# The first chunk's layer norm ahead of k's transposes, its token pairs inline, and its two turned tiles given to two engines

## The chip, the core and the metric

The kernel runs on one core of a Trainium2 chip. The metric is the time of one execution in microseconds (us). TensorE (PE in the profile) multiplies matrices and also transposes tiles by multiplying with an identity; its weight loads are listed apart as PEld. VectorE (DVE), ScalarE (ACT) and GpSimd (POOL) do the elementwise work, and SyncE (SP) and POOL issue the transfers (DMAs) that matter here. Each engine works through its own queue in order; engines wait for each other by semaphores.

## The reference

The program is a forward and a backward pass of a small network on x of 2048 tokens by 448 features, in bf16. Two layers, A and B, are each applied twice:

```
x = A_q
x = x + A(layernorm(x), A_k, A_v, A_shift_k, A_ssm_k, A_ssm_D)
x = x + B(layernorm(x), B_w1, B_w2)
x = x + A(layernorm(x), ...)          # the same weights again
x = x + B(layernorm(x), B_w1, B_w2)

A(q, k, v, ...):  k_shift = causal filter of k with 4 taps per feature
                  kv = k_shift * v
                  y  = long convolution of kv with ssm_k (2048 taps per feature, by FFT) + kv * ssm_D
                  return q * y
B(x, w1, w2):     silu(x @ w1) @ w2                       # 448 -> 1792 -> 448
```

The outputs are x and the gradients of A_q, A_k, A_v, A_shift_k, A_ssm_k, A_ssm_D, B_w1 and B_w2 for a given gradient of x. The convolution result Y does not depend on x, so it is computed once and used by both applications of A. The first application of A and the norm in front of B are, for every token, `na = layernorm(x)`, `X = x + na * Y`, `nb = layernorm(X)`.

## The kernel before

**Stages.** `_ssm_prefix` (L280) computes Y in about the first 105 us. After it, `Main.run` (L717) does the two layers forward and most of the backward pass, and `_ssm_suffix` the rest. The prefix is the part in which most of the change lies, and everything in `Main` needs its Y.

**The prefix, in order.** Tokens lie as 128 partitions by 16 (`J`), so that token 16p + j stands on partition p; a spectrum tile has 112 column groups of 128 (`SPEC`, 14336 columns), worked in 14 chunks of 1024 (`NCI`).

1. Loads: SP issues ssm_k in four pieces (`K_sb`), the FFT matrix `M1sb` and k (`kn`, which borrows the tile `Ysb`) in halves, v (`v_n`), and the inverse matrix `Minvsb`, 17.2 us from issue to landing for that last one. Then ssm_k is transposed (L334) and goes through stage one of the FFT (L211) into `A1K`.
2. k's transposes (L352 to L360): four groups of PSUM tiles `ps_kT`, each copied half by ACT and half by DVE into `kT`, which lies inside the tile `KB`.
3. The convolution loop (L404 to L415): eight rounds (two feature halves h, four token groups jq). In each, `conv` does the four-tap filter as 128-row matmuls with diagonal matrices (`ps_cv`, L371), ACT copies the result to `ks` (L373), POOL stores it to `KS_d`, and DVE multiplies with v to `kvt` (L377). `stage1_kv` (L381) takes the round before through stage one: two PSUM tiles, four copies into `A1kv`. In the first four rounds `turn` (L346) also transposes 16 tiles of `A1K` at a time and copies them to `Z` (two turns a round, 1.2 us on DVE or 1.9 on ACT each); in the last four `_fft_stage2` works on K's spectrum instead (two chunks of 1024 a round, copied to `Z` by `cons_ka`).
4. K's spectrum: POOL stores it to DRAM (`spec_K`), and `_swap_halves_dma` (L240) copies it, with its two halves of partitions exchanged, into `KB`: 14 transfers of 256 KB, written `KB<-Z` in the profile. They can start only when `kT`, which lies in `KB`, is no longer read. The last conv's reads and the last product with `v_n` are also what the loads of `w2sb` and, after `M1sb`, of `w1sb` wait for, since these reuse the buffers.
5. **The norm of the first chunk** (L421 to L424): POOL issues the load of the first four token columns of A_q (`x0c0`), and `_ln` normalises them into `na0`. `_ln` (L252) does, for four columns `tl`, a `bn_stats` (L259; with `pin` these are held in program order) and a `bn_aggr` on DVE, then adds epsilon (`ln_ve`, DVE), raises to the power -1/2 on POOL (`rstd`, L266), forms minus mean times rstd on DVE (`ln_nmr`, L268), and applies scale and bias per column (L273 on ACT, or a DVE instruction); last, POOL stores the result to `N_d`.
6. `A1kv` is turned into `Zkv` (which lies in `A1K`) in seven groups, and for each of 14 chunks `cons_prod` copies the spectrum of kv (ACT or DVE, in the profile `A1K` L111 or L113, from `ps_s`), multiplies it on DVE with K's spectrum (`pa`, L443) and with its swapped form (`pb`, L444), POOL stores every second chunk to `spec_KV`, and two chunks later PE takes the products through inverse stage two (`ps_v`, L231 and L232), whose result is copied to `A1kv`.
7. Inverse stage one (`ps_y`, L461): eight groups, copied to `Ysb` (the first by DVE, the rest by ACT).

**The first chunk in Main.** Under high priority, `a_fwd` makes `a_t1` = na0 * Y and X = x0c0 + a_t1 in two pairs of token columns, `b_pre` normalises X the same way (all on DVE) to `nb`, and `b_tr` turns it by 16 PE transposes in two tiles `ps_t`, each copied to a half of `nT`. Then `h` starts the MLP's first matmuls (`ps_h`, L519), which read `nT`.

**What sets the order.** The tile framework's scheduler orders the instructions into the queues by priority and modelled times; nothing is written out by hand here but the `pin` and the high priority. Which engine makes a copy is decided while the program is built: `bal.pick` (L93) adds an estimated cost to the less loaded of ACT and DVE, so moving or re-costing one item shifts later choices. Copies are recorded at L111 (ACT) and L113 (DVE) whoever calls for them. PSUM tiles of the prefix come from one ring of four (tag "A"); a PE group that takes the next buffer waits until the copy out of its former contents is done.

Of the kernel before, what the change touches and what calls it, by code (L numbers as in the profile page):

```python
# [11 lines left out]
BF16 = mybir.dt.bfloat16  # L12
ACT = mybir.ActivationFunctionType
ALU = mybir.AluOpType
# [3 lines left out]
P = 128  # L18
S = 2048
D = 448  # L20
# [88 lines left out]
def _copy(nc, eng, out, in_):  # L109
    if eng is nc.scalar:  # L110
        nc.scalar.copy(out, in_)  # L111
    else:
        eng.tensor_copy(out, in_)  # L113
# [101 lines left out]
def _fft_stage2(k, Zt, psum, consume, chunks=range(NCI)):  # L215
    nc = k.nc
    Zf = (Zt if isinstance(Zt, bass.AP) else Zt[:]).rearrange("q a b -> q (a b)")
    for ci in chunks:
        ps = psum.tile([P, 1024], FP32, name="ps_s2", **k.pt["s2"])
        for hh in range(2):  # L220
            c0 = ci * 1024 + hh * 512
            nc.tensor.matmul(ps[:, hh * 512:(hh + 1) * 512], lhsT=k.Gsb[:, G_FWD, :], rhs=Zf[:, c0:c0 + 512], start=True, stop=True)
        consume(ci, ps)
# [24 lines left out]
def _pm(ap2d):  # L248
    return ap2d.rearrange("(p j) d -> p j d", j=J)


def _ln(k, pool, c, src, si, n_g, groups=((0, 4),), pin=False, eng=None):  # L252
    nc = k.nc
    for lo, hi in groups:
        n = hi - lo
        st = pool.tile([P, 4, 6], FP32, name="ln_st", tag="ln_st", bufs=1)
        mv = pool.tile([P, 4, 2], FP32, name="ln_mv", tag="ln_mv", bufs=2)
        for tl in range(lo, hi):
            i = nc.vector.bn_stats(out=st[:, tl, :], in_=src(tl))  # L259
            if pin:  # L260
                k.tc.keep_in_program_order(i)
            nc.vector.bn_aggr(out=mv[:, tl, :], in_=st[:, tl, :])
        ve = pool.tile([P, 4], FP32, name="ln_ve", tag="ln_ve", bufs=2)
        nc.vector.tensor_scalar(out=ve[:, 0:n], in0=mv[:, lo:hi, 1], scalar1=EPS, scalar2=None, op0=ALU.add)
        r = k.rstd[si][:, 4 * c:4 * c + 4]
        nc.gpsimd.tensor_tensor(out=r[:, lo:hi], in0=ve[:, 0:n], in1=k.mhalf[:, 0:n], op=ALU.pow)  # L266
        nmr = pool.tile([P, 4], FP32, name="ln_nmr", tag="ln_nmr", bufs=2)
        nc.vector.scalar_tensor_tensor(out=nmr[:, lo:hi], in0=mv[:, lo:hi, 0], scalar=-1.0, in1=r[:, lo:hi], op0=ALU.mult, op1=ALU.mult)  # L268
        k.bal.add("dve", 0.8 * n + 0.2)
        for tl in range(lo, hi):  # L270
            e = eng or k.bal.pick(D, act_ns=1.04, dve_ns=0.55, act_fixed=0.28)
            if e is nc.scalar:
                nc.scalar.activation(n_g[:, tl, :], src(tl), ACT.Identity, bias=nmr[:, tl:tl + 1], scale=r[:, tl:tl + 1])  # L273
            else:
                nc.vector.tensor_scalar(out=n_g[:, tl, :], in0=src(tl), scalar1=r[:, tl:tl + 1], scalar2=nmr[:, tl:tl + 1], op0=ALU.mult, op1=ALU.add)
    if si != 2:
        nc.gpsimd.dma_start(out=_pm(k.N_d[si][:])[:, 4 * c:4 * c + 4, :], in_=n_g[:])


def _ssm_prefix(k):  # L280
    nc, tc = k.nc, k.tc
# [3 lines left out]
    with ExitStack() as es:  # L285
        spec = es.enter_context(tc.tile_pool(name="spec", bufs=1))
        work = es.enter_context(tc.tile_pool(name="pwork", bufs=2))
# [41 lines left out]
        for dc in range(ND):  # L329
            kview = ksb[dc].rearrange("p (n1 n2) -> p n2 n1", n2=16)  # L330
            pt = psum.tile([P, 2, 1024], BF16, name="ps_kt", **a_)
# [14 lines left out]
        def turn(src, dst, g):  # L346
# [2 lines left out]
                nc.tensor.transpose(pt[:, i, :], src[:, 16 * g + i, :], k.ident[:])  # L349
            _copy(nc, bal.pick(2048, dve_ns=0.53), dst[:, 16 * g:16 * g + 16, :], pt[:])  # L350

        for jq in range(4):  # L352
            pt = psum.tile([DC, ND, 4, P], BF16, name="ps_kT", **a_)
            for u in range(4):
                j = 4 * jq + u
                for dc in range(ND):
                    nc.tensor.transpose(pt[:, dc, u, :], kn[:, j, dc * DC:(dc + 1) * DC], k.ident[:])
            for e, lo, hi in ((nc.scalar, 0, 2), (nc.vector, 2, 4)):
                _copy(nc, e, kT[:, jq, lo:hi, :, 1:129], pt[:, lo:hi])
# [57 lines left out]
            _swap_halves_dma(k, KB, Ka, 2048 * i, 2048 * (i + 1), nc.gpsimd)  # L417
        stage1_kv(*prev)
        _fft_stage2(k, Z, psum, cons_ka, range(8, NCI))

        k.x0c0 = k.dp.tile([P, 4, D], BF16, name="x0c0", tag="dstat", bufs=3)  # L421
        nc.gpsimd.dma_start(out=k.x0c0[:], in_=_pm(k.A_q[0])[:, 0:4, :])
        k.na0 = k.dp.tile([P, 4, D], BF16, name="na0", tag="dstat", bufs=3)
        _ln(k, work, 0, lambda tl: k.x0c0[:, tl, :], 0, k.na0, pin=True)  # L424


        B1 = A1kv[:].rearrange("p a c n s -> p a (c n s)")
        Zf = A1K[:].rearrange("p a c n s -> p (a c n s)")
# [36 lines left out]
class Main:  # L465
# [52 lines left out]
            seen[u] = seen.get(u, 0) + 1  # L518
            self.nc.tensor.matmul(ps[:, u, :], lhsT=w[lo:hi, b, f:f + P], rhs=x[lo:hi, b, :], start=(seen[u] == 1), stop=(seen[u] == ND))  # L519

    def transp(self, src, dst):
        nc, k = self.nc, self.k
        blocks = [(0, 128), (128, 256), (256, 384), (320, 448)]
        rows = P
        for h in range(2):
            pt = k.psum.tile([P, 2, 512], BF16, name="ps_t", tag="tr", bufs=2)
            for u in range(2):
                lo, hi = blocks[2 * h + u]
                for tl in range(4):
                    nc.tensor.transpose(pt[:rows, u, tl * P:(tl + 1) * P], src[:, tl, lo:hi], k.ident[:])  # L530
            _copy(nc, k.bal.pick(1024, dve_ns=0.53), dst[:rows, 2 * h:2 * h + 2, :], pt[:rows])

    def a_fwd(self, c, si, xc, n_g=None, groups=((0, 4),)):
        nc, k, X = self.nc, self.k, self.X
        if n_g is None:
            n_g = self.ch.tile([P, 4, D], BF16, name="na", tag="na", bufs=2)
            src = (lambda tl: xc[:, tl, :]) if xc is not None else (lambda tl: X[:, 4 * c + tl, :])
            _ln(k, self.ch, c, src, si, n_g)
        t1 = self.ch.tile([P, 4, D], BF16, name="a_t1", tag="a_t1")
        for lo, hi in groups:  # L540
            sl = slice(4 * c + lo, 4 * c + hi)
            nc.vector.tensor_tensor(out=t1[:, lo:hi, :], in0=n_g[:, lo:hi, :], in1=self.Y[:, sl, :], op=ALU.mult)
            nc.vector.tensor_tensor(out=X[:, sl, :], in0=xc[:, lo:hi, :] if xc is not None else X[:, sl, :], in1=t1[:, lo:hi, :], op=ALU.add)
        k.bal.add("dve", 3.1)
        return n_g

# [3 lines left out]
        _ln(self.k, self.ch, c, lambda tl: X[:, 4 * c + tl, :], si, n_g, groups, eng=eng)  # L550
        return n_g

    def b_tr(self, n_g):
        nT = self.ch.tile([P, ND, 512], BF16, name="nT", tag="nT", bufs=2)
        self.transp(n_g, nT)
        return nT

    def slope(self, d, pieces=range(4)):
# [158 lines left out]
    def run(self):  # L717
        k, nc = self.k, self.nc
        pairs = ((0, 2), (2, 4))
        with self.tc.high_priority():  # L720
            self.a_fwd(0, 0, k.x0c0, k.na0, pairs)
            nT = self.b_tr(self.b_pre(0, 1, pairs, nc.vector))
        cur = []
        box = []

# [10 lines left out]
        for c in range(4):  # L736
            if c < 3:
                self.a_fwd(c + 1, 0, self.x0_load(c + 1))
                nb = self.b_pre(c + 1, 1)
            else:  # L740
                na, nb = self.a_fwd(0, 2, None), self.b_pre(0, 3)
            self.h(c, 0, nT, 1, cur)
            nT = self.b_tr(nb)
# [6 lines left out]
        for c in range(4):  # L750
# [19 lines left out]
            if c < 3:  # L770
                nb1 = box[0]
                nT = self.b_tr(nb1)
# [6 lines left out]
            na, nb = na1, nb1  # L779
# [327 lines left out]
```

## Time and profile before

| what | us |
|---|---|
| five runs | 754.16, 754.37, 754.48, 755.47, 763.88 |
| median | 754.48 |
| profiled execution | 757.87 |
| its span (first to last instruction recorded) | 755.7 |
| PE busy in it | 711.5 (94%) |
| DVE / ACT / POOL busy | 509.7 (67%) / 454.4 (60%) / 101.7 (13%) |
| mean granted PE clock | 0.989 of full |

Shares of the chain that ended last: PE 55%, DVE 18%, ACT 11%, DMA 9%, issue 5%.

The places around the change, by when they run in the profiled execution: k's transposes to about 27, the eight convolutions start at 27.47, 30.84, 34.97, 39.10, 42.17, 46.03, 49.43 and 52.83, the turn of `A1kv` starts at 61.21, the first `pa` at 69.89 and the last at 92.51, `ps_y` at 96.66, the last group of it at 104.92, and the first `ps_h` matmul at 110.42. The table gives busy time per stretch.

| stretch, us | PE | DVE | ACT | POOL | clock | DMA share |
|---|---|---|---|---|---|---|
| 12 to 24 | 10.53 | 6.95 | 8.79 | 0.00 | 1.00 | 1.02 |
| 46 to 58 | 11.36 | 10.01 | 9.99 | 4.62 | 1.00 | 0.58 |
| 58 to 70 | 10.51 | 11.55 | 10.61 | 5.77 | 1.00 | 1.04 |
| 87 to 100 | 8.58 | 6.82 | 7.57 | 2.65 | 0.77 | 1.03 |
| 100 to 107 | 5.48 | 5.92 | 5.70 | 1.19 | 0.94 | 0.33 |
| 107 to 116 | 7.13 | 4.15 | 5.88 | 2.03 | 0.62 | 1.21 |

How to read it: the stretch's length is the upper limit of a busy time. An engine that is full bounds the stretch; where none is full, the engines wait for each other. A clock of 0.77 says that TensorE ran at half speed in a part of the stretch. The DMA share is the mean busy share of the core's 16 DMA engines, about 1 where they are saturated (a little over 1 by the way it is measured). Groups of instructions are named by line, engine, and output<-input.

### The profile page before, as it was taken

To read this page: it belongs to the slowest core of one execution; us is meant where nothing else is said; L and a number is where in the kernel's file an instruction comes from. 1 tells how busy PE (TensorE), PEld (TensorE's weight loads), DVE (VectorE), ACT (ScalarE), POOL (GpSimd) and SP (SyncE) were. 2 spreads that over 40 slices of the span, in tenths; PEclk is the share of its full clock that TensorE was granted. 3 is DMA by queue.
4 is the path that set the end of the run, shared out by engine and by line. 5 is a ranking of instruction groups with operands and counts; after the bars stand their busy time and mean duration, and the time that the engine had idled before them with its cause. 6 is when DMAs were issued, how large, how long until landed. Compare 5 with 4: busy or idle time off the path is not lost.

```text
span 755.7 us, 12722 instructions
## 1 busy us (share of the span) xinstructions
PE 711.5 (94%) x5025; PEld 379.3 (50%) x5025; DVE 509.7 (67%) x1061; ACT 454.4 (60%) x572; POOL 101.7 (13%) x168
## 2 busy tenths in 40 slices
PE   5998779999999999999999999899999999999997
PEld 4886533444444443444434443344667675555554
DVE  3789858878733596985949989796487725199200
ACT  3878957667537588587677788547366754011111
POOL 1034312222100001000000000001111123111210
PEclk9999969999999999999999999999999999999999
DMA  9439989999969989868989999997758878487761
GB/s 291 171 130 276 349 265 290 290 308 239 239 155 234 220 211 248 193 154 197 207 227 299 247 285 264 281 241 253 271 221 326 290 278 265 147 310 220 214 185 46
DMA packets 188503, 180.17 MB, mean 238 GB/s; under 512 B 136154, under 2 KB 164702, under 8 KB 187292
## 3 DMA queue, kind: packets, MB, share of 16 engines
q1 hardware_dynamic: 174736, 122.21, 62.0%
q0 software_dynamic: 12784, 54.64, 20.6%
q10 hardware_dynamic: 924, 2.52, 1.0%
q8 instruction: 39, 0.64, 0.4%
q14 instruction: 20, 0.16, 0.1%
HBM read 76.66 MB, written 65.87 MB: 189 GB/s over the span
## 4 chain that ended last, share of the span: by engine, by line
PE 55%; DVE 18%; ACT 11%; DMA 9%; issue 5%; POOL 1%; SPq 0%; DVEq 0%; ACTq 0%; POOLq 0%
PE ps_d L822 21%; PE ps_h L519 8%; PE ps_o L602 6%; PE ps_n L675 3%; DMA GH_d<-turned 2%; DVE dT L113 2%; DVE lb_junk L650 2%; DMA turned<-ghT 2%; PE ps_g L519 2%; PE ps_v L232 2%; PE ps_v L231 2%; DVE lb_u L661 2%; ACT na L273 2%; PE ps_s L211 2%; DVE ln_st L259 1%
## 5 line engine op out<-in xcount | busy, mean ns | idle before, releaser
L822 PEld LDWEIGHTS <-dstat 128*128 128x128 bf16 x896 | 85.1, 98 | 73.0 <-issue 1.0
L519 PE MATMUL ps_h<-nT,w1sb 128*128 128x512 bf16 (+1 forms) x448 | 104.3, 387 | 2.6 <-DVE dT L113 1.4
L519 PE MATMUL ps_g<-gT,w2T 128*128 128x512 bf16 (+1 forms) x448 | 94.7, 381 | 5.0 <-ACT ghp L629 4.3
L675 PE MATMUL ps_n<-w1T,ghT 128*128 128x448 bf16 x448 | 91.3, 357 | 5.1 <-ACT lb_u L677 3.0
L602 PE MATMUL ps_o<-w2sb,aT 128*128 128x448 bf16 x448 | 91.0, 353 | 0.2 <-ACT aT L577 0.2
L822 PE MATMUL ps_d<-mov,dstat 128*128 128x448 bf16 x448 | 87.2, 352 | 0.5 <-DMA mov<-N_d 0.5
L577 ACT ACTIVATE aT<-ps_h 128x1024 bf16<-128x1024 f32 (+1 forms) x64 | 58.5, 918 | 43.8 <-PE ps_h L519 35.1
L113 DVE CAST dT<-ps_h 128x1024 bf16<-128x1024 f32 (+1 forms) x56 | 59.5, 1065 | 31.5 <-ACT aT L577 31.3
L519 PEld LDWEIGHTS <-w1sb 128*128 128x128 bf16 (+1 forms) x448 | 36.4, 97 | 66.2 <-issue 38.2
L519 PEld LDWEIGHTS <-w2T 128*128 128x128 bf16 (+1 forms) x448 | 35.1, 97 | 64.5 <-issue 32.4
L675 PEld LDWEIGHTS <-ghT 128*128 128x128 bf16 x448 | 42.6, 98 | 48.1 <-issue 6.2
L629 ACT CAST ghp<-ps_g 128x1024 bf16<-128x1024 f32 x56 | 55.5, 1006 | 17.5 <-PE ps_g L519 12.9
L602 PEld LDWEIGHTS <-aT 128*128 128x128 bf16 x448 | 42.0, 98 | 42.7 <-issue 4.8
L822 PE MATMUL ps_d<-GO,dstat 128*128 128x448 bf16 x224 | 51.4, 352 | 0.0
L822 PE MATMUL ps_d<-X,dstat 128*128 128x448 bf16 x224 | 50.5, 352 | 0.0
L865 ACT CAST dout<-ps_d 128x448 bf16<-128x448 f32 x14 | 7.5, 533 | 58.5 <-PE ps_d L822 58.5
L677 ACT ACTIVATE lb_u<-ps_n,rstd 128x448 f32<-128x448 f32 x32 | 20.3, 635 | 31.1 <-DVE X L662 15.4
L231 PEld LDWEIGHTS <-pa 128*128 128x128 bf16 x336 | 33.2, 99 | 10.3 <-DVE pa L443 6.7
L232 PEld LDWEIGHTS <-pb 128*128 128x128 bf16 x336 | 32.8, 99 | 9.5 <-DVE pb L444 4.8
L637 DVE TENSOR_TENSOR ghT<-dT,ghp 128x1024 bf16<-128x1024 bf16 (+1 forms) x32 | 19.5, 618 | 21.0 <-ACT ghp L629 18.8
L562 ACT ACTIVATE dTl<-dTl 128x1024 bf16<-128x1024 bf16 (+1 forms) x32 | 29.8, 946 | 5.5 <-DMA dTl<-DT_d 5.5
L603 DVE TENSOR_TENSOR X<-X,ps_o 128x448 bf16<-128x448 bf16 x32 | 19.7, 614 | 15.2 <-PE ps_o L602 15.1
(192 smaller groups left out, 1206.8 us busy)
## 6 DMA issues: line engine op xcount, KB each, us to landing
GH_d<-turned SPq DMA_DIRECT2D x16, 896.0 KB, 5.7
dstat<-A_d SPq DMA_DIRECT2D x28, 512.0 KB, 5.6
dstat<-GH_d SPq DMA_DIRECT2D x28, 512.0 KB, 3.9
A_d<-turned SPq DMA_DIRECT2D x12, 896.0 KB, 4.9
DT_d<-dT POOLq DMA_DIRECT2D x8, 896.0 KB, 6.7
dTl<-DT_d SPq DMA_DIRECT2D x8, 896.0 KB, 6.1
spec_K<-Z POOLq DMA_DIRECT2D x7, 512.0 KB, 7.5
KB<-Z POOLq DMA_DIRECT2D x14, 256.0 KB, 12.4
```

Source lines behind the costliest of these rows:

```text
L113: eng.tensor_copy(out, in_)
L231: nc.tensor.matmul(pv[:, i, :], lhsT=pa[:, i * P:(i + 1) * P], rhs=k.Gsb[:, ga, :], start=True, stop=False)
L232: nc.tensor.matmul(pv[:, i, :], lhsT=pb[:, i * P:(i + 1) * P], rhs=k.Gsb[:, gb, :], start=False, stop=True)
L519: self.nc.tensor.matmul(ps[:, u, :], lhsT=w[lo:hi, b, f:f + P], rhs=x[lo:hi, b, :], start=(seen[u] == 1), stop=(seen[u] == ND))
L562: self.k.last_slope = self.nc.scalar.activation(s, s, ACT.Derivative_silu)
L577: last = nc.scalar.activation(a, ps[:, 0:n, :], ACT.Silu)
L602: nc.tensor.matmul(po[:, :D], lhsT=aT[ft // 7][0][:, ft % 7, tl * P:(tl + 1) * P], rhs=self.w2sb[:, ft, :], start=(ft == 0), stop=(ft == N ...
L603: nc.vector.tensor_tensor(out=X[:, t, :], in0=X[:, t, :], in1=po[:, :D], op=ALU.add)
L629: k.last_gh = nc.scalar.copy(gh[:], ps[:])
L675: mm = nc.tensor.matmul(pn[:, :D], lhsT=ghT[ft // 7][:, ft % 7, tl * P:(tl + 1) * P], rhs=self.w1T[:, ft, :], start=(ft == 0), stop=(ft == ...
L677: last_u = nc.scalar.activation(u0[:], pn[:, :D], ACT.Identity, scale=k.rstd[2 * L + 1][:, t:t + 1], accum_out=cp[:, tl, 0:1])
L822: i = k.nc.tensor.matmul(ps[:, :D], lhsT=st[:, t, :], rhs=mov[:, t, :], start=start and t == 0, stop=stop and t == NT - 1)
```

## The change

Four edits:

- `x0c0`'s load and the first chunk's `_ln` stand ahead of k's transposes instead of after K's stage two; the load is issued by SP instead of POOL.
- In `Main.run` gate, addition and `_ln` of the first chunk are written out by pairs of token columns, instead of both pairs' gates first and then both pairs' norms. The store of `nb` stays a single one (`store=hi == 4`). `a_fwd` loses the arguments that only the first chunk used, and with them that chunk's `bal.add("dve", 3.1)`.
- `transp` and `b_tr` take a pair of engines: the first chunk's first `ps_t` is copied by ACT and the second by DVE, instead of both by the balancer's choice (ACT for both).
- By the first edit the balancer sees the norm's cost before the convolution loop, so a number of copies of the prefix change engine.

```diff
@@ -249,7 +249,7 @@
     return ap2d.rearrange("(p j) d -> p j d", j=J)
 
 
-def _ln(k, pool, c, src, si, n_g, groups=((0, 4),), pin=False, eng=None):
+def _ln(k, pool, c, src, si, n_g, groups=((0, 4),), pin=False, eng=None, store=True):
     nc = k.nc
     for lo, hi in groups:
         n = hi - lo
@@ -273,7 +273,7 @@
                 nc.scalar.activation(n_g[:, tl, :], src(tl), ACT.Identity, bias=nmr[:, tl:tl + 1], scale=r[:, tl:tl + 1])
             else:
                 nc.vector.tensor_scalar(out=n_g[:, tl, :], in0=src(tl), scalar1=r[:, tl:tl + 1], scalar2=nmr[:, tl:tl + 1], op0=ALU.mult, op1=ALU.add)
-    if si != 2:
+    if si != 2 and store:
         nc.gpsimd.dma_start(out=_pm(k.N_d[si][:])[:, 4 * c:4 * c + 4, :], in_=n_g[:])
 
 
@@ -349,6 +349,10 @@
                 nc.tensor.transpose(pt[:, i, :], src[:, 16 * g + i, :], k.ident[:])
             _copy(nc, bal.pick(2048, dve_ns=0.53), dst[:, 16 * g:16 * g + 16, :], pt[:])
 
+        k.x0c0 = k.dp.tile([P, 4, D], BF16, name="x0c0", tag="dstat", bufs=3)
+        nc.sync.dma_start(out=k.x0c0[:], in_=_pm(k.A_q[0])[:, 0:4, :])
+        k.na0 = k.dp.tile([P, 4, D], BF16, name="na0", tag="dstat", bufs=3)
+        _ln(k, work, 0, lambda tl: k.x0c0[:, tl, :], 0, k.na0, pin=True)
         for jq in range(4):
             pt = psum.tile([DC, ND, 4, P], BF16, name="ps_kT", **a_)
             for u in range(4):
@@ -418,12 +422,6 @@
         stage1_kv(*prev)
         _fft_stage2(k, Z, psum, cons_ka, range(8, NCI))
 
-        k.x0c0 = k.dp.tile([P, 4, D], BF16, name="x0c0", tag="dstat", bufs=3)
-        nc.gpsimd.dma_start(out=k.x0c0[:], in_=_pm(k.A_q[0])[:, 0:4, :])
-        k.na0 = k.dp.tile([P, 4, D], BF16, name="na0", tag="dstat", bufs=3)
-        _ln(k, work, 0, lambda tl: k.x0c0[:, tl, :], 0, k.na0, pin=True)
-
-
         B1 = A1kv[:].rearrange("p a c n s -> p a (c n s)")
         Zf = A1K[:].rearrange("p a c n s -> p (a c n s)")
 
@@ -518,7 +516,7 @@
             seen[u] = seen.get(u, 0) + 1
             self.nc.tensor.matmul(ps[:, u, :], lhsT=w[lo:hi, b, f:f + P], rhs=x[lo:hi, b, :], start=(seen[u] == 1), stop=(seen[u] == ND))
 
-    def transp(self, src, dst):
+    def transp(self, src, dst, engs=None):
         nc, k = self.nc, self.k
         blocks = [(0, 128), (128, 256), (256, 384), (320, 448)]
         rows = P
@@ -528,19 +526,17 @@
                 lo, hi = blocks[2 * h + u]
                 for tl in range(4):
                     nc.tensor.transpose(pt[:rows, u, tl * P:(tl + 1) * P], src[:, tl, lo:hi], k.ident[:])
-            _copy(nc, k.bal.pick(1024, dve_ns=0.53), dst[:rows, 2 * h:2 * h + 2, :], pt[:rows])
-
-    def a_fwd(self, c, si, xc, n_g=None, groups=((0, 4),)):
+            _copy(nc, engs[h] if engs else k.bal.pick(1024, dve_ns=0.53), dst[:rows, 2 * h:2 * h + 2, :], pt[:rows])
+
+    def a_fwd(self, c, si, xc):
         nc, k, X = self.nc, self.k, self.X
-        if n_g is None:
-            n_g = self.ch.tile([P, 4, D], BF16, name="na", tag="na", bufs=2)
-            src = (lambda tl: xc[:, tl, :]) if xc is not None else (lambda tl: X[:, 4 * c + tl, :])
-            _ln(k, self.ch, c, src, si, n_g)
+        n_g = self.ch.tile([P, 4, D], BF16, name="na", tag="na", bufs=2)
+        src = (lambda tl: xc[:, tl, :]) if xc is not None else (lambda tl: X[:, 4 * c + tl, :])
+        _ln(k, self.ch, c, src, si, n_g)
         t1 = self.ch.tile([P, 4, D], BF16, name="a_t1", tag="a_t1")
-        for lo, hi in groups:
-            sl = slice(4 * c + lo, 4 * c + hi)
-            nc.vector.tensor_tensor(out=t1[:, lo:hi, :], in0=n_g[:, lo:hi, :], in1=self.Y[:, sl, :], op=ALU.mult)
-            nc.vector.tensor_tensor(out=X[:, sl, :], in0=xc[:, lo:hi, :] if xc is not None else X[:, sl, :], in1=t1[:, lo:hi, :], op=ALU.add)
+        sl = slice(4 * c, 4 * c + 4)
+        nc.vector.tensor_tensor(out=t1[:], in0=n_g[:], in1=self.Y[:, sl, :], op=ALU.mult)
+        nc.vector.tensor_tensor(out=X[:, sl, :], in0=xc[:] if xc is not None else X[:, sl, :], in1=t1[:], op=ALU.add)
         k.bal.add("dve", 3.1)
         return n_g
 
@@ -550,9 +546,9 @@
         _ln(self.k, self.ch, c, lambda tl: X[:, 4 * c + tl, :], si, n_g, groups, eng=eng)
         return n_g
 
-    def b_tr(self, n_g):
+    def b_tr(self, n_g, engs=None):
         nT = self.ch.tile([P, ND, 512], BF16, name="nT", tag="nT", bufs=2)
-        self.transp(n_g, nT)
+        self.transp(n_g, nT, engs)
         return nT
 
     def slope(self, d, pieces=range(4)):
@@ -718,8 +714,13 @@
         k, nc = self.k, self.nc
         pairs = ((0, 2), (2, 4))
         with self.tc.high_priority():
-            self.a_fwd(0, 0, k.x0c0, k.na0, pairs)
-            nT = self.b_tr(self.b_pre(0, 1, pairs, nc.vector))
+            t1 = self.ch.tile([P, 4, D], BF16, name="a_t1", tag="a_t1")
+            n_g = self.ch.tile([P, 4, D], BF16, name="nb", tag="nb", bufs=2)
+            for lo, hi in pairs:
+                nc.vector.tensor_tensor(out=t1[:, lo:hi, :], in0=k.na0[:, lo:hi, :], in1=self.Y[:, lo:hi, :], op=ALU.mult)
+                nc.vector.tensor_tensor(out=self.X[:, lo:hi, :], in0=k.x0c0[:, lo:hi, :], in1=t1[:, lo:hi, :], op=ALU.add)
+                _ln(k, self.ch, 0, lambda tl: self.X[:, tl, :], 1, n_g, ((lo, hi),), eng=nc.vector, store=hi == 4)
+            nT = self.b_tr(n_g, (nc.scalar, nc.vector))
         cur = []
         box = []
 
```

## The prediction

> **What bounds the kernel now.** I read the page's busy shares first: PE is busy 711.5 of 755.7 us, so time lost early, with PE kept waiting, is not made up later. The change touches about 20 to 116 us. There the view of stretches shows which engine has room:
>
> ```profile
> 24.00:36.00 12.00, 12.00 (x224) 12.00 (x222) 8.77 (x13) 9.27 (x10) 1.54 (x2) 1.00 0.27 90
> 36.00:46.00 10.00, 9.86 (x152) 8.90 (x149) 7.82 (x12) 7.50 (x11) 2.11 (x3) 1.00 0.17 48
> ...
> 70.00:87.00 17.00, 15.33 (x183) 10.41 (x183) 16.69 (x26) 16.36 (x18) 6.39 (x10) 1.00 1.04 299
> ```
>
> The columns are PE, PEld, DVE, ACT, POOL, the clock, the DMA share and GB/s. From 24 to 46 (convolution) PE has no gap and DVE and ACT have some 5 us each. From 70 to 87 (inverse transform) DVE, ACT and the DMA engines are all full. Then I followed the chain that ended last, and DVE's timeline at the same place:
>
> ```profile
> 87.15 2.60 ACT na L273 x4
> 89.75 0.90 ACT A1K L111
> ```
> ```profile
> 86.59 0.69 DVE L444 TENSOR_TENSOR pb<-A1K,KB 128x1024 bf16<-128x1024 bf16 x1 [0.24 <-DMA KB<-Z]
> ...
> 87.80 0.68 DVE L444 TENSOR_TENSOR pb<-A1K,KB 128x1024 bf16<-128x1024 bf16 x1
> 90.69 0.69 DVE L443 TENSOR_TENSOR pa<-A1K,Z 128x1024 bf16<-128x1024 bf16 x1 [2.21 <-ACT A1K L111]
> 91.30 0.68 DVE L444 TENSOR_TENSOR pb<-A1K,KB 128x1024 bf16<-128x1024 bf16 x1
> ```
>
> The four normalisations on ACT stand in front of the twelfth spectrum's copy (counted from zero), DVE waits 2.21 us for it, and PE behind it. So the moved work does cost time where it is. Note the first line: another pb waited for a swap transfer, KB<-Z. The DMA view of the last swap's issue gives its landing, 77.05 + 13.0 = 90.05:
>
> ```profile
> KB<-Z POOLq DMA_DIRECT2D x1, 256.0 KB, 13.0
> ```
>
> **Parts that cost nothing.** *Token pairs:* in the trace DVE already runs both gates (99.47, 100.78), both adds, then the statistics (102.39); the changed program's queue has the same order, and one store either way. 0 us. *Load of x0c0, from POOL to SP:* POOL loses an issue of 0.58 us at 5.84 and is then idle to 30.29. On SP it stands behind Minvsb (landed 10.12 + 17.2 = 27.3) and before w2sb, which waits to 56.23 anyway. The same 448 KB left the same saturated engines before (landed 14.2), so the stream ends when it did, and x0c0 lands at about 27.3; the first statistics are due at 28.4. Bounds: Minvsb gains the 1.1 us that 448 KB take at the 417 GB/s of the stretch 12 to 24, or x0c0 comes 1.1 us late, just in time. 0 us at both ends. *Store of na0:* moves on POOL from 90.04 to about 38, where the DMA share is 0.17; it stood behind the last swap, so it frees nothing waited for. 0 us.
>
> **Step 1, the cost in the convolution.** Added on DVE: 4 bn_stats at 0.53 from start to start, 4 aggregates at 0.09, ve and nmr, 2.7 us; on ACT 4 x 0.65 = 2.6 us. By busy time both fit. But queues run in order, and I walked the changed program's queues with this trace's durations. bn_stats goes ahead of DVE's fourth kT copy; with three more around kvt, the copy of the first turned tile on DVE ends at 33.25 instead of 31.78, and PE, whose next stage-one tile needs that buffer, stops 0.45 us. ve ends at 33.5. nmr waits for POOL's power: from ve's start to nmr's start took 1.33 us at 110.00, 1.8 if the first power takes 1.52 us as at 79.58 instead of 1.03. So nmr starts at 34.7 to 35.2. Behind it on DVE queue the A1kv copy, kvt, a second A1kv copy (0.54 each) and the turned tile's copy (1.21), which now ends at 37.6 to 38.1. The third convolution takes its buffer. It started at 34.97 and now starts at 37.6 to 38.1: **2.7 to 3.1 us late**.
>
> On ACT the four normalisations run from 34.9 (35.4) to 37.5 (38.0); behind them two A1kv copies and the 1.87 us turned copy, on which the next transposes wait (40.2 to 40.7 instead of 37.15). So 3.1 to 3.6 late. In the second half the copies are shared out differently: each round becomes convolution 1.65, ks 0.93, kvt 0.56, A1kv copy 0.64, together 3.78, against PE's 3.40 (49.43, 52.83) now; two rounds add 0.75. The last kvt comes 3.5 to 3.9 us late, and with it w2sb's load and the swaps. On PE part is won back at the tail, and the transposes at 61.21 start 2.8 to 3.3 late.
>
> **Step 2, clock.** A PE stall of 2.2 to 2.7 us may also cost clock:
>
> ```profile
> 87.18:90.59 3.41, 2.08 (x31) 1.74 (x31) 1.30 (x3) 3.41 (x6) 0.55 (x2) 1.00 1.02 351
> 90.59:94.00 3.41, 1.60 (x20) 1.17 (x21) 2.78 (x5) 2.81 (x4) 2.10 (x4) 1.00 1.03 420
> 94.00:97.42 3.42, 2.32 (x18) 1.71 (x17) 0.94 (x1) 1.01 (x1) 0.00 (x0) 0.50 1.02 418
> 104.24:107.66 3.42, 1.24 (x8) 0.37 (x6) 2.80 (x11) 1.88 (x3) 1.21 (x2) 1.00 0.33 65
> 646.99:650.40 3.41, 2.07 (x15) 1.14 (x15) 1.69 (x16) 0.28 (x1) 0.00 (x0) 1.00 0.02 5
> ```
>
> Cut at its clock changes, the trace halves the clock after stretches of 3.41 us with PE busy 1.60 or 1.24, not after 2.07. At the trace's phase PE would be busy 1.3 to 1.7 between 35.98 and 39.39, on the slow side. The next stretch at half speed stretches a stage-one pair (0.77) and a transposed tile (0.9): 1.1 us, what the ring of copies leaves of it. Bounds 0 and 1.1; I take 0.7.
>
> [...]
>
> **Step 3, the gain in the inverse transform.** From 62.76 to 69.96 DVE loses the same 2.7 us, but the first pa at 69.89 also needs ACT's copy, started 68.53: only 0.33 us comes back. At 86.19 nmr goes, where a swap bounds the next pb anyway (86.5). At 87.03 ACT loses 2.6 us. What is late next? The last swap: its pb ran at 91.30, and its data were there at 90.05, so **only 1.25 us** of the 2.6 can be had. After it the last pair ran at 92.51, 93.12 because its spectrum's copy came late on ACT; without that it follows at once, 0.6 us sooner. Gain 1.85. But the DMA engines have been full since 57 (share 1.04), so the swaps land as late as they were fed: 3.5 to 3.9 us. Cost less gain at ps_y: 1.65 to 2.05 us late (98.3 to 98.7 instead of 96.66).
>
> **Step 4, turned tiles by two engines.** ACT's second nT copy (110.38 to 111.29) goes to DVE behind two bn_stats, 109.9 to 110.6. PE's third matmul waited for it to 111.34, having been able to go at about 111.28 at half clock or 110.85 at full: gain 0.1 to 0.45. DVE's next nmr comes some 0.65 later (0.69 more in front of it), where ACT has 0.9 in hand: 0. I take 0.3.
>
> **Sum.** 1.85 - 0.3 + 0.7 = 2.25; at the low ends 1.65 - 0.45 + 0 = 1.2, at the high ends 2.05 - 0.1 + 1.1 = 3.05. I take 2.0, a little below, since the slow stretches after 94 absorb some of a shift. The profiled execution took 757.87 us (span 755.7 and 2.2 around it) and would take 759.9. The median of the runs is 3.4 lower; the same sum gives 754.48 + 2.0 = **756.5 us**, own range 755.2 to 757.8. That is 0.27% slower, and less than the 1% that a measurement here can tell from no change.
>
> **Rivals.**
> *The convolution absorbs the norm (faster).* For it: 5 us of free time on both engines, and the planner gave PE another buffer for the third convolution. Against it: nmr's wait at DVE's head. If the swaps come less than about 2 us late the sign turns; at 0 late the time is 1.85 + 0.3 better, 752.3.
> *The inverse stage keeps full clock.* If the 1.6 us gaps around the last swap fall across two windows, ps_v (1.70 against 0.95) and eight ps_y (3.16 against 1.60) run at full rate, 2.3 us better than the sum: 754.2. For it: PE was busy 1.60 in the deciding window, near the edge. Against it: the gap for the last swap remains.
> *One slow stretch more (slower).* A pair of slow stretches where now is one (the gate opened at 100.83 only after 3.41 us of unbroken work; ps_y starting 1.85 us late breaks that) costs half of 3.41, 1.7 us over the high end: 754.48 + 3.05 + 1.0 to 1.7, about 758.9. It decides if PE's start falls after 97.42 and the stretch behind it isn't full.
> *The pairs do nothing and the move cancels:* within 0.5 of 754.5, inside the second rival.
>
> **Chances.** Forecast 0.48, absorbed 0.17, full clock 0.17, one stretch more 0.16, something else 0.02. The range takes all but the outer halves of the two extreme rivals: 752.3 to 758.6. Faster by over 1% 0.01, within 1% 0.97, slower by over 1% 0.02.
>
> **What would show it.** Right: DVE's nmr at 34.7 to 35.2 with POOL as releaser; the third ps_cv group on PE near 38 after a wait for DVE's Z copy; rounds of 3.8 us; w2sb issued near 60; the last pb waiting for KB<-Z; ps_y at 98 to 99. Wrong: no PE gap at 35 to 38 (step 1 falls, the time is near 752), or the last swap landing before 92 although fed late (step 3's DMA bound falls).

## The result, and the profile after

The changed kernel took 757.94 us (median of 54 runs), the kernel before 755.42 us (median of 94, those shown above among them). The ratio is 1.0032, 95% interval 1.0021 to 1.0042: **1.6 to 3.2 us slower**, where 2.0 had been forecast. The forecast of 756.5 us stood on the median of five runs, 754.48; on that of all 94 the same 2.0 gives 757.4, and the measured time lies 0.5 us above it. The profiled execution took 757.77 us, its span 756.0.

A single profile says little about that, since its first loads, its clock and some places further on differ from execution to execution by more than the effect (e1_load and e12_load below, the same program, are 2.2 us apart from the first convolution to the first `ps_h`, and another 5.9 from there to the first `ps_g`). So most readings below are distances within one profile, above all from the first convolution on PE to a later point. The first view is the one of stretches of the changed kernel, with the columns of the prediction (PE, PEld, DVE, ACT, POOL, the clock, the DMA share and GB/s):

```profile
24.00:36.00 12.00, 9.93 (x177) 9.65 (x176) 9.52 (x20) 9.34 (x11) 2.62 (x3) 1.00 0.21 72
36.00:46.00 10.00, 9.57 (x140) 9.29 (x140) 5.38 (x10) 7.40 (x9) 1.96 (x3) 0.83 0.20 71
```

PE had no gap between 24 and 36 before; now 2 us are missing, though neither DVE nor ACT is full. From 36 to 46 the clock is 0.83: a stretch at half speed that was not there. The timeline of PE shows the gap, that of DVE what precedes it:

```profile
32.39 1.95 PE L349 MATMUL ps_tr<-ident,A1K 128*128 128x128 bf16 x32
36.43 2.48 PE L375 MATMUL ps_cv<-KB 112*128 112x112 bf16 x32 [2.09 <-DVE Z L113]
38.70 1.70 PE L391 MATMUL ps_s<-kvt,M1sb 128*128 128x224 bf16 x8
40.20 2.15 PE L349 MATMUL ps_tr<-ident,A1K 128*128 128x128 bf16 x32
```
```profile
33.48 0.16 DVE L268 SCALAR_TENSOR_TENSOR ln_nmr<-ln_mv,rstd 128x4 f32<-128x4 f32 x1 [1.24 <-POOL rstd L266]
...
35.16 1.21 DVE L113 COPY Z<-ps_tr 128x2048 bf16<-128x2048 bf16 x1
39.70 1.15 DVE L113 CAST A1kv<-ps_s 128x448 bf16<-128x448 f32 x2 [3.32 <-PE ps_s L391]
```

In before the same two steps of PE took:

```profile
34.80 1.74 PE L371 MATMUL ps_cv<-KB 112*128 112x112 bf16 x32
36.38 0.93 PE L387 MATMUL ps_s<-kvt,M1sb 128*128 128x224 bf16 x8
```

The third convolution (`ps_cv`) waits 2.09 us for DVE's copy `Z`, which stands behind nmr, which waits 1.24 us for POOL's power. The convolution then takes 2.48 us instead of 1.74 and the stage-one pair 1.70 instead of 0.93: that is the half clock (0.50 from 37.20 to 40.61). The chain of waits near the end of the inverse transform:

```profile
75.96 15.15 DMA KB<-Z
...
91.20 0.70 DVE pb L442
...
93.77 1.01 ACT A1kv L111
94.78 0.92 ACT A1K L111
95.71 0.02 issue
95.73 0.69 DVE pa L441
```

A swap transfer issued at 75.96 lands at 91.11, and the product waits for it. Behind it on ACT stands `A1kv` (the copy of that product's transform) and behind that in ACT's queue the last spectrum's copy `A1K`, for which the last `pa` waits. In before, the four `na` on ACT stood in ACT's queue one spectrum earlier, in front of the last but one.

| us after the first convolution | before | changed |
|---|---|---|
| third convolution | 7.49 | 10.32 |
| last convolution | 25.52 | 30.89 |
| first `pa` | 42.58 | 46.99 |
| last `pb` | 65.81 | 70.23 |
| first `ps_y` | 69.35 | 73.08 |
| first `ps_h` | 83.11 | 85.38 |

The norm costs 5.37 us up to the last convolution, less than 1 us of it comes back up to the first `pa`, and from there to the last `pb` both take some 23.2 us. Another 0.7 us comes back up to `ps_y`, and 1.5 us in `ps_y` itself, which took 6.23 us instead of 8.26, because the clock was full there (1.00 from 95.22 to 108.88); in before it was at half (0.50) from 94.00 to 100.83.

### The profile page after: what moved, and what is told of

It is laid out like the page before. It is cut to its first block, busy times and chain, and to the rows that moved or that the text cites. A ratio compares the mean times of both kernels' runs of the same rounds, so it can differ in the third digit from the quotient of the medians.

```text
span 756.0 us, 12727 instructions
## 1 busy us (share of the span) xinstructions
PE 709.0 (94%) x5025; PEld 380.5 (50%) x5025; DVE 510.0 (67%) x1062; ACT 452.3 (60%) x571; POOL 100.5 (13%) x167
## 4 chain that ended last, share of the span: by engine, by line
PE 50%; DVE 21%; ACT 10%; DMA 5%; issue 4%; POOL 1%; DVEq 0%; ACTq 0%; POOLq 0%
PE ps_d L823 21%; PE ps_h L517 8%; PE ps_o L598 6%; DMA KB<-Z 3%; PE ps_n L671 3%; DVE lb_junk L646 3%; DVE lb_u L657 2%; DVE dT L113 2%; PE ps_g L517 2%; DVE ghT L633 2%; PE ps_v L232 2%; PE ps_v L231 2%; DVE lb_u L687 2%; DVE ln_st L259 1%; ACT ghp L625 1%
## 5 line engine op out<-in xcount | busy, mean ns | idle before, releaser
L573 ACT ACTIVATE aT<-ps_h 128x1024 bf16<-128x1024 f32 (+1 forms) x64 | 58.5, 917 | 43.2 <-PE ps_h L517 34.7
L633 DVE TENSOR_TENSOR ghT<-dT,ghp 128x1024 bf16<-128x1024 bf16 (+1 forms) x32 | 19.5, 618 | 20.9 <-ACT ghp L625 20.8
```

Source lines behind the costliest of these rows:

```text
L573: last = nc.scalar.activation(a, ps[:, 0:n, :], ACT.Silu)
L633: nc.vector.tensor_tensor(out=ghT[hh][:, o:o + len(u), :], in0=dT[hh][1][:, o:o + len(u), :], in1=gh[:, u[0]:u[0] + len(u), :], op=ALU.mult)
```

## The experiments

Ratios are to the kernel before, run beside them on the same chip, with their 95% intervals. All interpretations use this table of distances from the first convolution, each from one profile:

| kernel | last convolution | `ps_y` | `ps_h` | ratio |
|---|---|---|---|---|
| before | 25.52 | 69.35 | 83.11 | |
| e1_load, e12_load | 25.52, 25.51 | 68.67, 69.43 | 80.97, 83.20 | 1.0020 (0.9997 to 1.0044), 1.0003 (0.9981 to 1.0024) |
| e3_turns | 25.52 | 69.18 | 81.49 | 0.9984 (0.9960 to 1.0008) |
| changed | 30.89 | 73.08 | 85.38 | 1.0032 (1.0021 to 1.0042) |
| e2_norm | 31.59 | 73.44 | 85.75 | 1.0030 (1.0005 to 1.0056) |
| e6_nmr | 29.84 | 70.80 | 83.12 | 1.0039 (1.0015 to 1.0063) |
| e7_swaps | 29.74 | 69.36 | 82.06 | see there |
| e5_bal | 28.01 | 69.43 | 81.74 | 1.0007 (0.9988 to 1.0026) |
| e9_balnmr | 28.10 | 69.15 | 81.20 | 1.0005 (0.9986 to 1.0025) |
| e4_pool, e10_pool | 26.09, 26.60 | 67.16, 67.90 | 79.53, 80.02 | 0.9977 (0.9949 to 1.0006), 0.9972 (0.9949 to 0.9995) |
| e8_poolload, e11_poolload | 25.52, 25.52 | 66.90, 66.78 | 79.28, 79.16 | 0.9941 (0.9917 to 0.9965), 0.9941 (0.9918 to 0.9965) |

### The parts alone

e2_norm is before with the first edit alone:

```diff
+        k.x0c0 = ...; nc.sync.dma_start(out=k.x0c0[:], ...)   # ahead of k's transposes
+        k.na0 = ...; _ln(k, work, 0, ..., k.na0, pin=True)
-        (load on POOL and _ln behind K's stage two)
```

> Load and norm of the first chunk ahead of k's transposes, without the pairs and without the second engine for the turned tiles. Theory 'the whole loss comes from the norm in the convolution stage': as the changed kernel, plus 0.3 us for the second nT copy back on ACT, ratio 1.003 to 1.004; third convolution on PE after a wait of about 2 us for DVE's Z copy. Rival 'the pairs or the second engine cost time': ratio below 1.002.

Ratio 1.0030, and every distance within 0.7 us of the changed kernel's. The loss is in the first edit. The 0.70 us by which its last convolution is later than the changed kernel's are there at the third convolution already (11.02 us after the first, against 10.32), because DVE's first statistic waited for the load:

```profile
26.16 0.63 DVE L259 BATCH_NORM_STATS2 ln_st<-x0c 128x6 f32<-128x448 bf16 x1 [0.60 <-DMA x0c<-in_A_q_dram]
```

e3_turns is before with the other two edits alone (pairs written out, `self.b_tr(n_g, (nc.scalar, nc.vector))`).

> Only the token pairs written out and the turned tiles on two engines; the prefix is that of before. Theory: the third ps_h matmul no longer waits for ACT's second copy, gain 0.1 to 0.45 us, ratio 0.9994 to 0.9999. Rival 'the second copy on DVE delays the next chunk's norm by 0.65 us and PE waits for it': ratio 1.000 to 1.001.

Its interval holds both theories. Its profile is finer: between the first and the third `ps_h` matmul lie 0.92, 0.91, 0.92 and 0.92 us in the four profiles with both copies on ACT (before, e2, e1, e12) and 0.80 us in the changed kernel and in e3. So the gain is about 0.12 us, the low end of 0.1 to 0.45, and from `ps_h` to `ps_o` (the MLP's second matmuls) e3 (4.76) is no longer than e1 (4.79).

e1_load and e12_load are the same kernel, before with only the load moved to SP:

```diff
+        k.x0c0 = ...; nc.sync.dma_start(out=k.x0c0[:], ...)   # ahead of k's transposes
-        k.x0c0 = ...; nc.gpsimd.dma_start(out=k.x0c0[:], ...) # behind K's stage two in the text
```

> The load of x0c0 alone goes to SP behind Minvsb; the norm stays in its old place. Theory 'the load was in the way of the first loads': 448 KB less in front of ssm_k, M1sb, k and v, so the first convolution on PE starts 0.5 to 1.2 us sooner than the 27.31 of before, and the time falls by as much, ratio 0.9985 to 0.9993. Rival 'the 1.2 us by which the changed kernel's profile starts its convolutions sooner is the luck of one execution': the first convolution near 27.3, ratio 1.000.

> Before with only the load moved to SP, a second time. Theory 'the first loads come sooner': ratio 0.9990 to 0.9995. Rival 'worth nothing': 1.000. If the first time's 1.002 was a real loss: 1.001 to 1.003.

No gain: the mean of the two ratios is 1.0011, give or take 0.0016. From the first transpose to the first convolution, the ten profiles with the load on SP took 19.83 to 21.88 us, the four with it on POOL 21.03 to 21.90. The ranges overlap, and the means (20.9 and 21.4) are 0.5 us apart; how much of the 1.2 us by which the changed kernel's profile was ahead at the first convolution is the load's doing, and how much the scatter of the first loads, is not shown.

### What the norm costs in the convolution

e4_pool finishes the norm on POOL, and leaves DVE the statistics and ACT nothing:

```diff
+        if on_pool:
+            for tl in range(lo, hi):
+                nc.gpsimd.tensor_scalar(out=n_g[:, tl, :], in0=src(tl), scalar1=mv[:, tl, 0:1],
+                    scalar2=r[:, tl:tl + 1], op0=ALU.subtract, op1=ALU.mult)
+            continue
```

> The changed kernel, but the first chunk's norm is finished on POOL: (x minus mean) times rstd, four instructions, so DVE has no nmr that waits for POOL's power and ACT has no normalisation; the copies stay with the engines they had in before. Theory 'nmr at the head of DVE's queue and the four normalisations on ACT make the loss': no PE wait of 2 us at the third convolution (0.5 us at most at the second turn), last convolution at most 1.5 us later against the first than in before (it is 5.4 later in the changed kernel), swaps and ps_y sooner, ratio 0.996 to 0.999. Rival 'the statistics alone, or the load, make the loss': ratio 1.002 to 1.004. Rival 'POOL's four instructions take long and hold up the stores, or slow DVE': the fourth round late by their length.

Three things go with this at once: DVE's nmr, ACT's normalisations, and, since the `continue` skips it, what the balancer is told of the norm. The last convolution is 0.57 us late instead of 5.37, and the kernel is faster than before by all but the edge of the interval. POOL's timeline of e4_pool shows that these instructions are slow, and the stores to `KS_d` and `N_d` behind them wait:

```profile
32.68 7.72 POOL L269 TENSOR_SCALAR na<-x0c,ln_mv,rstd 128x448 bf16<-128x448 bf16 x4
40.35 0.86 POOL L383 DMA_DIRECT2D KS_d<-ks  x1
```

That is 1.93 us each, against some 0.65 on ACT, on an engine that has only stores to issue there: the convolutions do not notice.

So DVE's wait for POOL, or ACT's normalisations? e6_nmr takes away only the wait: DVE makes a negated mean beforehand, POOL multiplies it with its own power.

```diff
+            nc.vector.tensor_scalar(out=negm[:, lo:hi], in0=mv[:, lo:hi, 0], scalar1=-1.0, ..., op0=ALU.mult)
-        nc.vector.scalar_tensor_tensor(out=nmr[:, lo:hi], in0=mv[:, lo:hi, 0], scalar=-1.0, in1=r[:, lo:hi], ...)
+            nc.gpsimd.tensor_tensor(out=nmr[:, lo:hi], in0=negm[:, lo:hi], in1=r[:, lo:hi], op=ALU.mult)
```

> The changed kernel with nmr made on POOL behind the power (a negated mean is made on DVE before), so DVE has no instruction that waits for POOL; the four normalisations stay on ACT. Theory 'both waits matter': the third convolution starts 4.1 to 4.7 us after the second (4.13 in before, 6.95 in the changed kernel), no stretch at half clock there; but ACT's normalisations still hold its copies, so the last convolution comes 27 to 29 us after the first (25.5 in before, 30.9 in the changed kernel); ratio 1.000 to 1.002. Rival 'only nmr's wait matters': last convolution 26.1 after the first as with all of it on POOL, ratio 0.998. Rival 'only ACT's normalisations matter': the third convolution 6 us or more after the second.

The third convolution came 5.63 us after the second, between 4.13 and 6.95, so none of the three forecasts (4.1 to 4.7, 26.1 at the end, 6 or more) was met: the wait was not all of it. What was saved there was lost one step later, when PE's next transposes waited 1.22 us for ACT's `Z` copy behind the four normalisations. The last convolution is at 29.84, and at 29.74 in e7_swaps, which has the changed kernel's instructions here, nmr on DVE included, and no half clock. So **nmr's wait costs nothing at the end**. The ratio of 1.0039 is larger than its `ps_h` explains; its profiled execution (752.68 us) was the fastest of its twelve, whose median is 756.84.

e5_bal keeps the norm on ACT and DVE but sets the balancer back to what it held before the norm:

```diff
+        was = dict(bal.load)
         _ln(k, work, 0, ..., k.na0, pin=True, eng=nc.scalar)
+        bal.load = was
```

> The changed kernel, the norm on ACT as there, but the balancer is set back to what it held before the norm, so that the copies of the prefix go to the engines they had in before. Theory: the wait of 2 us at the third convolution stays; from the fourth convolution to the eighth it takes 13.9 us as in before instead of 14.8, so ps_y starts 0.5 to 1 us sooner against the first convolution (72.1 to 72.6 instead of 73.1) and the ratio is 1.001 to 1.003. Rival 'the wait at the third convolution makes the slower rounds too': 14.8 stays.

From the fourth to the eighth convolution it took 13.70 us, as the theory had it, but the third came sooner too (5.83 us after the second instead of 6.95). `ps_y` is 3.65 us sooner, far more than the 0.5 to 1 expected: 1.15 us are the half clock, 1.73 the copies themselves (29.74 to 28.01), and the rest is won in the inverse stage. With the copies on their old engines and the norm where the change puts it, the loss is 1.0007, no longer measurable.

e9_balnmr does both:

```diff
+        was = dict(bal.load)
         _ln(k, work, 0, ..., k.na0, pin=True, nmr_pool=True, eng=nc.scalar)
+        bal.load = was
```

> Both mends of the norm on ACT at once: the balancer set back (copies on the engines they had in before) and nmr behind the power on POOL. The last convolution came after the first by 30.9 us in the changed kernel, 29.8 with nmr on POOL alone, 28.0 with the balancer set back alone, 25.5 in before. Theory 'three separate costs, the copies 2.9, nmr 1.1, ACT's normalisations the rest': 26.9 to 27.0, ps_y 68.4 to 69.0 after the first convolution, ratio 0.997 to 1.000. Rival 'with ACT's normalisations in front, DVE's wait is covered': 28.0 as without it, ratio 1.000 to 1.001.

28.10: the rival holds, nmr's wait is covered here too. The timelines of ACT and PE of e9_balnmr show by what:

```profile
34.80 2.73 ACT L279 ACTIVATE na<-x0c,ln_nmr,rstd 128x448 bf16<-128x448 bf16 x4 [1.43 <-POOL ln_nmr L272]
37.43 0.51 ACT L111 CAST A1kv<-ps_s 128x448 bf16<-128x448 f32 x1
37.84 1.86 ACT L111 COPY Z<-ps_tr 128x2048 bf16<-128x2048 bf16 x1
```
```profile
35.21 1.74 PE L383 MATMUL ps_cv<-KB 112*128 112x112 bf16 x32
36.78 0.55 PE L399 MATMUL ps_s<-kvt,M1sb 128*128 128x224 bf16 x4
38.65 0.54 PE L399 MATMUL ps_s<-kvt,M1sb 128*128 128x224 bf16 x4 [1.32 <-DVE A1kv L113]
39.75 1.95 PE L355 MATMUL ps_tr<-ident,A1K 128*128 128x128 bf16 x32 [0.56 <-ACT Z L111]
```

The third convolution has no wait at all, but ACT itself waits 1.43 us for POOL and then works 2.73 us on the norm, the next `A1kv` copies come late (DVE's follow ACT's), and PE stops two instructions later.

Put together, the 5.37 us by which the last convolution is late are:

| cost | us | from |
|---|---|---|
| statistics behind k's copies on DVE | 0.57 | e4 26.09 less 25.52 (e10: 1.08) |
| ACT waiting for POOL and normalising | 1.92 | e5 28.01 less e4 26.09 |
| DVE's nmr waiting for POOL | 0 | e9 against e5, e6 against e7 |
| copies that the balancer moved | 1.73 | e7 29.74 less e5 28.01 |
| a stretch at half clock | 1.15 | changed 30.89 less e7 29.74 (e2, from the third convolution on: 1.15 more than e7, too) |

Each is a difference of two profiles; e5's DVE queue also has one copy in another order than before's.

### The swaps

e7_swaps is the changed kernel with the two weight loads taken from beside the swaps:

```diff
-    nc.sync.dma_start(out=k.w1sb[...], ...)  # and w2sb
+    with tc.issue_after(k.last_swap.ins):
+        nc.gpsimd.dma_start(out=k.w1sb[...], ...)  # and w2sb
```

> The changed kernel, but w1sb and w2sb are loaded by POOL behind the last swap transfer instead of by SP beside the swaps (3.2 MB less beside them). Theory 'the swaps' landing on full DMA engines ends the inverse stage': no pb waits for KB<-Z any more, the last pb comes 1.5 to 3 us sooner (67.2 to 68.7 after the first convolution instead of 70.2), ps_y too; ratio 0.998 to 1.001 if the weights are there in time for ps_h. Rival 'the swaps land late only because they are fed late': the waits for KB<-Z stay near 2.4 us in all, ratio 1.003.

DVE's timeline of e7_swaps, at the last products:

```profile
89.40 0.68 DVE L443 TENSOR_TENSOR pb<-A1K,KB 128x1024 bf16<-128x1024 bf16 x1
90.11 0.69 DVE L442 TENSOR_TENSOR pa<-A1K,Z 128x1024 bf16<-128x1024 bf16 x1
90.72 0.68 DVE L443 TENSOR_TENSOR pb<-A1K,KB 128x1024 bf16<-128x1024 bf16 x1
91.95 0.69 DVE L442 TENSOR_TENSOR pa<-A1K,Z 128x1024 bf16<-128x1024 bf16 x1 [0.54 <-ACT A1K L111]
```

No product waits for a swap any more, where the changed kernel waited 1.72 and 0.68 us. The last swap took 7.3 us from issue to landing instead of 13.0, and from the first `pa` to the last `pb` it took 20.66 us instead of 23.23. The theory of the full DMA engines (share 1.04 from 70 to 87 in the changed kernel) holds, for the swaps. As a version it is none: its six runs took 757.47 to 774.58 us, and the ratio is 1.0126 (1.0066 to 1.0186), where 0.998 to 1.001 had been expected. Why is not shown. In its profile, of its fastest run, it took 128.55 us from the first `ps_h` to the first `ps_g`, a matmul group further on, instead of 124.23, with a wait of ACT of 8.76 us for `turned<-aT`, a transfer of Main. But e12_load, which loads the weights as before does, took 129.94 us there and waited 5.32 and 3.79 us for the same transfer, where the same program in e1_load took 124.04. So this profile does not show that the moved weight loads are the reason.

### The load's place, once the norm is on POOL

e8_poolload (and e11_poolload, the same) is e4_pool with `nc.gpsimd.dma_start` for `x0c0`, as in before; e10_pool is e4_pool again.

> The kernel that finishes the norm on POOL, but with x0c0's load on POOL at the front as in before. Theory 'the load in front of the stream delays the first loads': from the first transpose to the first convolution 0.5 to 1.2 us more than the 20.65 of the kernel with the load on SP, ratio 0.998 to 1.0005. Rival 'the load's place is worth nothing': 20.7, ratio 0.996 to 0.998 as with the load on SP.

> The kernel that finishes the norm on POOL, x0c0 loaded by SP, a second time beside the next one. Theory 'the load behind the stream helps': 0.3 to 0.6 us faster than the next one. Rival 'its place is worth nothing, or the load by POOL is the better': the same or slower. Against before 0.994 to 0.998 by either.

> The kernel that finishes the norm on POOL, x0c0 loaded by POOL at the front, a second time. From its start of ps_y (66.9 us after the first convolution against some 69 in before) and 0.1 to 0.3 for the turned tiles: ratio 0.9965 to 0.9975; if the first time's 0.9941 was more than scatter, 0.993 to 0.996.

The theory that the load on SP helps fell: the load on POOL is the better, 0.9941 both times, below both forecasts made for e8_poolload. DVE's timeline of e8_poolload shows what it changes in the convolution:

```profile
23.51 0.62 DVE L259 BATCH_NORM_STATS2 ln_st<-x0c 128x6 f32<-128x448 bf16 x1
24.33 0.69 DVE L113 COPY KB<-ps_kT 112x1024 bf16<-112x1024 bf16 x1 [0.20 <-ACT KB L111]
24.94 0.17 DVE L262 BATCH_NORM_AGGREGATE ln_mv<-ln_st 128x2 f32<-128x6 f32 x1
25.03 0.59 DVE L259 BATCH_NORM_STATS2 ln_st<-x0c 128x6 f32<-128x448 bf16 x1
```

and that of e10_pool what happens with the load on SP:

```profile
25.32 0.69 DVE L113 COPY KB<-ps_kT 112x1024 bf16<-112x1024 bf16 x1 [0.22 <-ACT KB L111]
26.44 0.63 DVE L259 BATCH_NORM_STATS2 ln_st<-x0c 128x6 f32<-128x448 bf16 x1 [0.42 <-DMA x0c<-in_A_q_dram]
```

With the data there early, the planner puts the statistics between k's copies, where DVE waits 0.22 us per copy for ACT anyway, and the last convolution comes 25.52 us after the first, exactly as with no norm there. From SP, behind Minvsb, they come after three of the four copies and even wait for the load. That is worth 0.57 to 1.08 us, some 0.1%. The ratios (mean 0.9941 against 0.9975, each give or take 0.0018) say 0.3%, with a margin that reaches from 0.1 to 0.6%; what more there may be, the profiles do not show, and it is left open.

So the fastest version is the norm finished on POOL with the load on POOL: **0.9941 (0.9918 to 0.9965)** of before, about 4.4 us.

## Why the prediction held, and where its terms were off

**Step 1, the convolution: 2.7 to 3.1 at the third, 3.5 to 3.9 at the end.** The third convolution was 2.83 us late, and nmr started at 33.48 in a profile whose first convolution is 1.20 ahead, so at 34.7 in the terms of the prediction; the last two rounds took 3.96 and 3.97 us where 3.78 had been walked (3.40 in before), and `w2sb` was issued at 60.36. At the end, without half clock, 4.22 (e7). So the size was right at the third convolution and 0.3 us too small at the end. The reason given first, nmr at the head of DVE's queue, is true of the third convolution and of nothing after it; the ACT side of the step (3.1 to 3.6) is what carries through. And the rounds, put at 0.75, were part of a larger item, the copies that the balancer moves (1.73). The walk through the queues counted most of this, but as consequences of the norm's own work, and only setting the balancer back (e5) showed that the norm by itself, where it stands, costs hardly more than it gains (ratio 1.0007).

**Step 2, the clock: 0 to 1.1, taken as 0.7.** Measured 0 (e7) and 1.15 (changed, and e2 from its third convolution on) with the same instructions: the two bounds were right, and each profile shows one of them, none the 0.7 between. Which of the two it was went with where the gap fell in the windows, the stretches of 3.41 us on whose grid the clock changes of a profile lie. The windows of the changed kernel, then of e7_swaps:

```profile
33.79:37.20 3.41, 1.32 (x26) 1.20 (x24) 2.58 (x4) 3.41 (x7) 0.94 (x2) 1.00 0.22 70
37.20:40.61 3.41, 3.41 (x32) 3.13 (x30) 0.91 (x2) 2.65 (x3) 0.52 (x2) 0.50 0.36 139
```
```profile
32.32:35.73 3.41, 1.96 (x34) 1.84 (x33) 2.31 (x5) 2.11 (x4) 1.81 (x2) 1.00 0.22 68
35.73:39.15 3.42, 2.66 (x43) 2.50 (x43) 1.21 (x3) 3.42 (x5) 0.56 (x1) 1.00 0.35 136
```

The same gap of 2 us lies within one window in the first and across two in the second: it began 0.6 us after a window's start in one execution and 2.0 us after it in the other. PE was busy for 1.32 us of that one window, and the next ran at 0.50; of the other two it was busy for 1.96 and 2.66 us, and the window behind them (39.15 to 42.56) ran at 1.00.

**Step 3, the gain: 1.85, capped by the swaps.** From the last convolution to `ps_y` the four profiles with the norm in its old place took 43.15 to 43.92 us (mean 43.6), the changed kernel 42.19, e2 41.85: a gain of 1.5 and 1.8. Some of that is clock: e1 and e2, both at full clock all the way there, differ by 1.3 (43.15 and 41.85). The cap was real: the last swap landed at 81.25 + 13.0 = 94.25, which is 68.1 us after the first convolution, 5.4 later than in before (90.05, 62.7) and just as late as the last convolution (5.37); where the swaps land early (e7), the same stretch took 39.6 us instead of 42.19. Two details were wrong. The 0.6 us between the last two pairs was not won (1.96 us between their `pb`, before 1.82), since ACT's last spectrum copy now waits behind a copy that itself depends on the late swap. Up to the first `pa` 0.96 us came back rather than 0.33.

**Step 4: 0.12 instead of 0.3**, within its bounds.

**The load at 0 us** was the term that the sum lacked: its place decides where the statistics fit, 0.57 to 1.08 us of which step 1 counted only a stop of 0.45. Nor was it always in time: in e2 and e10, two of the eight profiles with the load on SP and the norm early, the first statistic waited 0.60 and 0.42 us for it. The bound "x0c0 comes 1.1 us late, just in time" asked whether the data arrive before the first statistic, not where the planner could otherwise have put it.

**The sum.** `ps_h` came 83.1, 81.0, 81.5 and 83.2 us after the first convolution in the four profiles with the norm in its old place (mean 82.2), 85.4 and 85.8 in the two with it moved: 3.4 late, where the runs say 1.6 to 3.2 and 2.5 in the middle; the difference is within what single profiles scatter (81.0 to 83.2 for one and the same inverse stage). The steps had 2.25 and the forecast 2.0. That the total came so near is in part luck. `ps_y` came 73.1 and 73.4 us after the first convolution against a mean of 69.2, some 4.1 late where steps 1 to 3 had 2.55; in the terms of the prediction, which has the first convolution at 27.31, that is 100.4 in the changed kernel, where it gave 98 to 99 as a sign of being right. The excess in the convolution was met in part by the second rival, the inverse stage at full clock. Of those four, three had a stretch at half clock between 85 and 101 us, of the ten with the norm elsewhere only one, the changed kernel's (91.81 to 95.22), over before `ps_y`. The rows of e12_load (norm in its old place) around ACT's four normalisations:

```profile
89.90:93.31 3.41, 1.25 (x17) 0.94 (x17) 2.05 (x4) 3.41 (x4) 2.61 (x5) 1.00 1.03 419
93.31:96.72 3.41, 2.06 (x16) 1.71 (x17) 1.67 (x2) 1.12 (x2) 0.04 (x1) 0.50 1.03 422
```

ACT is full with the normalisations and PE busy for only 1.25 us; the next 6.83 us run at half speed. The gap of PE behind them, 1.85 to 2.21 us in the four profiles, is gone in eight of the ten others, where the longest gap there is 1.29 us. In the changed kernel and e2 a wait for a swap takes its place (1.75 and 2.18 us). Behind the first of these came the stretch at half clock that was over before `ps_y` (PE busy 1.50 us from 88.40 to 91.81), behind the second none; that `ps_y` ran at full clock in these two was, by the author's estimate, also a matter of where the gap fell. It is a rival whose effect was added to the forecast's rather than taking its place. The rival "the convolution absorbs the norm" failed for the change as made, and is what e8_poolload does. The slower rival, one stretch more behind `ps_y`, did not show.

## What to carry to other kernels

Moving work to where two engines have free time by the table is not free when it enters queues that run in order (5.37 us at the last convolution here): price it where it stands in each queue, and look for an idle engine that can take it even at three times the duration (POOL at 1.93 us against 0.65 on ACT made a loss a gain). A balancer that is told of the moved work re-deals everything behind it (1.73 us here); compare with its state set back before blaming the work itself. When data must be there for filler work, load it early enough that the filler can sit in gaps that exist, not merely before its first use (0 us at the last convolution that way, 0.57 and 1.08 us otherwise).

## What the runs showed of the hardware

- What the clock did went with how long PE was busy in the 3.41 us before. In each profile the clock changes up to 740 us lie on one grid of 3.41 us. Cut at it, and without the program's first and last microseconds, before has 210 stretches at full clock: three were followed by half clock, with PE busy 1.17, 1.24 and 1.60 us, and the others had 2.05 or more. The changed kernel has 211: 0.57, 1.32 and 1.50 us in the three, 1.80 or more in the others. The fourteen profiles together have some 2940: 27 were followed by half clock, all with PE busy 1.67 us or less, and of the others only two had less than 1.77 (both 1.5). A PE gap of some 2 us inside busy work cost 1.15 us more in the changed kernel, and nothing more in e7_swaps, with the same instructions.
- Two executions of one program differ by microseconds at places where a transfer is waited for. From the first `ps_n` matmul to the first `ps_d` e4 and e10, the same code, took 256.46 and 259.51 us; ACT's longest wait for `dTl<-DT_d` there was 2.1 and 5.2 us. From the first `ps_h` to the first `ps_g` e1 and e12, again the same code, took 124.04 and 129.94 us; in e12 ACT waited 5.32 and 3.79 us for `turned<-aT`.
- The last 256 KB swap took 13.0 us from issue to landing beside two weight loads (changed kernel) and 7.3 without them (e7_swaps).
